# First unit's receptance product from split weights, and a new written order for the first units

## The chip, the cores and the metric

The kernel runs on one core of a Trainium2 chip. The metric is the device time of one execution in microseconds (us). The kernel before took 607.07 us, the median of three runs (606.57 to 607.09). Its engines are TensorE (PE, with its weight loads as PEld), VectorE (DVE), ScalarE (ACT), GpSimd (POOL) and SyncE (SP), which issues every DMA of this kernel.

## What is computed

The reference is sliding-window attention followed by a channel-mixing block. Batch 8, 8 heads, 576 positions, head size 64; window 64; then `d_model` 512 and `d_ff` 1024.

```python
scores = q @ k.T / sqrt(64), kept where 0 <= i - j < 64
attn   = exp(scores - max) / (sum + 1e-9)
x      = attn @ v                       # (8, 576, 512), heads side by side
x_prev = x shifted by one position, first one zero
xk = mu_k * x + (1 - mu_k) * x_prev
xr = mu_r * x + (1 - mu_r) * x_prev
k  = relu(xk @ w_k);  v = (k * k) @ w_v
out = sigmoid(xr @ w_r) * v
```

The weights are stored as 64-bit floats, so the kernel has to turn them into 32-bit ones ("decode") on the chip before it can use them.

## The kernel before, in words

**Units.** The 4608 positions are worked in 9 units of 512 positions (`NU`, `TU`). Each unit has four attention groups g (`NC` = 4 channel chunks of 128), so unit 0 has g0 to g3 and unit 1 has g4 to g7. For one group: scores on PE (`run_s`), per block a masked minimum on DVE (`least`) and an exponential on ACT (`exp`), the reciprocal sums on DVE (`shares`), a scaling on POOL or DVE (`scale`), a transposition of the weights (for unit 0 PE transposes, `flip`, with a copy out on ACT or DVE; later units use DVE's `turn`), the product with v on PE (`run_x`) and the copy of x to SBUF.

**Mixing.** Per unit and chunk c, `mix` (L873) makes xr and xk: `diff` (any of three engines), `blend` (DVE), and, where the product is a split one, `high` (a cast to fp32r, ACT or POOL) and `low` (the rest, a subtraction on DVE or POOL).

**Products.** `product` (L951) makes a 128x512 output from `count` chunks. A *split* product is three fp32r matmuls for each chunk: high weight by high x, high by low, low by high. A *whole* one is one fp32 matmul for each chunk, which needs neither `high` nor `low` of x nor the two parts of the weight; the trace has two records for it. `direct` (L484) decides: with `DIRECT = "rk"` unit 0 takes w_r and w_k whole, and all else is split. Unit 0 has 4 x 4 r products (r0 to r3, chunks c0 to c3), 8 x 4 k products and 4 x 8 v products.

**Weights.** 20 chunks n of 512 KB are loaded: n0 to n3 are w_r, n4 to n11 w_k, n12 to n19 w_v. `decode` (L421) takes each through `sign` (ACT), `clamp` (DVE or POOL), `shift`, `top`, `low` (DVE), then `first_part` (a cast, ACT or POOL) and `second_part` (a subtraction, POOL or DVE), which give the split weight. Where a chunk is used whole in unit 0, `low` writes a tile `whole` that stays, and the two parts are made at any time before unit 1.

**Order.** Every step is a numbered `Piece`. `play` (L206) walks through a model of the engines and gives each engine its order of instructions. For the beginning the orders are written out: `ORDER` (L90) lists for each engine the piece numbers in the order in which it issues them; what is not listed there follows by the model's own choice, with assumed costs. Engines run their own list in order and wait for each other by semaphores. `PLACES` (L81) names the pairs of groups (j, groups 2j and 2j+1) ahead of whose `run_x` PE's instruction addresses are aligned by no-operations. `BOUND` (L46) is the model time up to which a POOL piece is also ordered behind the last DVE piece that shares a port with it.

Of the kernel before, what the change touches and what calls it, by code (L numbers as in the profile page):

```python
# [42 lines left out]
SB = 14  # L43

ORDERED = mybir.DependencyInfo(mybir.DependencyClass.Sync, mybir.DependencyReason.DATA)
BOUND = 125000  # L46

GATES = 1
LATER = (4,)

DIRECT = "rk"
SPLIT = (-9, -47)
WHOLE = 859

# [23 lines left out]
LINK = {"DVE": 125, "ACT": 135, "POOL": 90, "PE": 205, "SP": 80}  # L78
FAR_LINK = 45

PLACES, SKIP = {3: 7, 4: 7, 8: 7, 12: 7, 16: 7}, 12  # L81

RING = 8
FIRST = 730
# [4 lines left out]

ORDER = {  # L90
# [9 lines left out]
    ),  # L100
    "DVE": (
# [11 lines left out]
    ),  # L113
    "ACT": (
# [10 lines left out]
    ),  # L125
    "POOL": (
# [4 lines left out]
    ),  # L131
# [7 lines left out]
    ),  # L139
}  # L140

# [6 lines left out]
def attn_rwkv_kernel(ctx, tc, qT, kT, v2, mu_k, mu_r, w_k, w_v, w_r, out):  # L148
# [57 lines left out]
    def play():  # L206

        left, free, now, begun, port, bus, landed, run = {}, {}, 0, [], 0, 0, [], None
        holder = None
        moved, clock, tiled = 0, [WINDOW, 0, True], None  # L210
# [34 lines left out]
        while any(left.values()) or any(script.values()):  # L245
            assert times, [(e, [(p.key, p.fn.__name__) for _, _, p in ps[:4]]) for e, ps in left.items()]
            now = heapq.heappop(times)
            while ends and ends[0][0] <= now:
                _, _, p = heapq.heappop(ends)
# [4 lines left out]
            for e, ps in left.items():  # L254
# [3 lines left out]
                for _, n, p in ([(0, 0, given[-1])] if given else ps):  # L258
# [37 lines left out]
                    if locks:  # L296
                        port = p.done
# [4 lines left out]
                    if p.size:  # L302
                        early = moved < 1.034e6
                        bus, moved = max(bus, now - 335), moved + p.size
                        bus += 36 + p.size / (352.6 if early else 376.6) + 178 * (early and p.size > 5e5)
                        landed.append(bus + (2132 if early else 3373))
                        p.lag = landed[-1] - p.done + (1500 if bus > 16000 else 300)
                        heapq.heappush(times, landed[-1])
                    if e == "PE":
# [8 lines left out]
    def d1(n):  # L318
        return 65 + 1.04 * n

    def d2(n):
        return 65 + 0.52 * n
# [658 lines left out]
    def r_units(key, u, xr, gate, n=TU):  # L981
        made, hold = [x[2] for x in xr], [x[1] for x in xr]

        for m in range(NC):
            ps, held, p = product(key, wr_s, m, lambda c, e: xr[c][0][0] if e is None else xr[c][0][0][:, e], made, lambda c: [hold[c]], NC, n,
                                  spare=u > 0, u=u)
            state, scratch, result = [], Hold("tmp"), Hold("r")
# [25 lines left out]
            p = Piece("ACT", key, 2 * act_ns(n) + 20, powers, [p], [scratch, result], held)  # L1013
            if u < GATES:
                p = Piece("ACT", key + LATER[0], 2 * cast_ns(n) + 16, bounded, [p])
            p = Piece("DVE", key + (LATER[0] if u < GATES else 0), (0 if u < GATES else 2 * d2(n)) + d1(n), share, [p], uses=[scratch], port=True)
            gate.append((state, result, p))

    def k_units(key, u, xk, k2, n=TU):
# [109 lines left out]
    for j in range(PAIRED // 2, len(groups) // 2):  # L1129
        u = 2 * j // NC  # L1130
# [79 lines left out]
```

## Time and profile before

| what | value |
|---|---|
| median of three runs | 607.07 us (606.57 to 607.09) |
| the profiled execution | 607.59 us |
| its span, first to last instruction | 605.8 us |
| PE busy | 593.6 us (98%) |
| DVE busy | 391.1 us (65%) |
| ACT busy | 371.3 us (61%) |
| POOL busy | 133.9 us (22%) |
| granted TensorE clock, mean | 0.999 |

The span is one execution; 1.79 us of the execution's time lie outside it. Shares are means over the whole span: the stages differ much, with DVE and ACT nearly full over the first 100 us and half empty later. In the views a line is nearly always L168, since all instructions go through one helper there, so the names of the tiles say what a row is: `bank<-xm,whole` is a whole product, `bank<-xs,ws` or `bank<-ks,ws` a split one, `bank<-qk` scores, `bank<-ident,pr` PE transposes, `bank<-pt,v` attention times v.

### The profile page before, as it was taken

The page shows a single profiled execution, that of the slowest core. Times are in us where ns is not written, and L with a number is a line of the kernel's source. Part 1 is how long each engine was busy: PE and PEld are TensorE (multiplying, and loading weights), DVE is VectorE, ACT ScalarE, POOL GpSimd, SP SyncE. Part 2 cuts the span into 40 slices and gives each one's busy share as a digit, 9 for nine tenths or more (in the row PEclk, how much of TensorE's full clock was granted, in tenths as well). Part 3 has the DMA queues.
Part 4 walks back from the last instruction along what each step waited for, and adds up shares of the span by engine and source line. Part 5 has one row for each costly group of instructions (what it writes and reads, how often), then busy time and mean ns, then how long its engine had stood idle before and what let it go on. Part 6 is the DMA issues. An engine that isn't in the chain of part 4 may idle for free.

```text
span 605.8 us, 17561 instructions
## 1 busy us (share of the span) xinstructions
PE 593.6 (98%) x7008; PEld 464.7 (77%) x7008; DVE 391.1 (65%) x1210; ACT 371.3 (61%) x1057; POOL 133.9 (22%) x205
## 2 busy tenths in 40 slices
PE   5999999999999999999999999999999999999997
PEld 4644577888888888888888888887888888888885
DVE  5999999737782768366754677277828683665211
ACT  6898967475576646673577358645865476743620
POOL 6665546202300330022101130023002300201000
PEclk9999999999999999999999999999999999999999
DMA  8988133213221323122312222132212220010001
GB/s 276 320 287 282 47 88 105 80 45 107 83 77 46 93 75 97 40 82 63 110 40 57 88 83 66 41 110 81 75 46 93 92 81 24 3 53 18 0 18 52
DMA packets 56913, 53.32 MB, mean 88 GB/s; under 512 B 10496, under 2 KB 50432, under 8 KB 56832
## 3 DMA queue, kind: packets, MB, share of 16 engines
q1 hardware_dynamic: 56832, 52.20, 28.2%
q8 instruction: 56, 0.92, 0.6%
q14 instruction: 25, 0.20, 0.1%
HBM read 42.73 MB, written 9.44 MB: 86 GB/s over the span
## 4 chain that ended last, share of the span: by engine, by line
PE 84%; DVE 6%; ACT 4%; DMA 3%; SPq 1%; issue 1%; POOL 1%; ACTq 0%
PE bank L168 84%; DVE bank L168 1%; DMA raw<-w_k 1%; ACT pr L168 1%; SPq L168 1%; DMA v<-v 1%; DMA raw<-w_r 1%; DVE xm L168 1%; ACT ws L168 1%; DVE wt L168 1%; ACT kf L168 1%; DVE d L168 1%; DVE r L168 0%; DVE whole L168 0%; DVE pt L168 0%
## 5 line engine op out<-in xcount | busy, mean ns | idle before, releaser
L168 PE MATMUL bank<-xs,ws 128*128 128x512 f32 x1152 | 272.7, 396 | 0.0
L168 PEld LDWEIGHTS bank<-xs,ws 128*128 128x128 f32 x1152 | 215.8, 188 | 51.0
L168 PE MATMUL bank<-ks,ws 128*128 128x512 f32 x864 | 206.8, 398 | 0.1
L168 PEld LDWEIGHTS bank<-ks,ws 128*128 128x128 f32 x864 | 161.3, 188 | 39.5 <-issue 1.0
L168 DVE TENSOR_TENSOR ks<-kf,ks 128x512 fp32r<-128x512 f32 x70 | 51.3, 734 | 93.7 <-ACT ks L168 93.5
L168 ACT ACTIVATE pr<-pr,nmax 128x96 f32<-128x96 f32 (+1 forms) x288 | 105.2, 368 | 8.8 <-DVE nmax L168 8.3
L168 ACT ACTIVATE kf<-bank 128x512 f32<-128x512 f32 x72 | 43.0, 598 | 61.1 <-PE bank L168 60.7
L168 DVE CUSTOM_DVE_ANT_0 pr<-bank,bands 128x96 f32<-128x96 f32 x256 | 49.5, 250 | 14.3 <-PE bank L168 14.3
L168 POOL CAST ks<-kf 128x512 fp32r<-128x512 f32 x7 | 4.3, 612 | 244.9 <-ACT kf L168 206.0
L168 ACT COPY xT<-bank 128x256 f32<-128x256 f32 (+1 forms) x43 | 14.5, 392 | 67.0 <-PE bank L168 67.0
L168 ACT ACTIVATION_READ_ACCUMULATOR pr<-pr,nmax 128x1 f32 x288 | 54.5, 189 | 0.0
L168 ACT ACTIVATE kf<-kf 128x512 f32<-128x512 f32 x71 | 44.8, 633 | 2.0
L168 ACT ACTIVATE th<-bank 128x512 f32<-128x512 f32 x36 | 21.3, 591 | 38.5 <-PE bank L168 27.2
L168 DVE SCALAR_TENSOR_TENSOR r<-bank,r 128x512 f32<-128x512 f32 x36 | 24.4, 680 | 31.4 <-PE bank L168 31.3
L168 PE MATMUL bank<-xm,whole 128*128 128x512 f32 x96 | 43.1, 599 | 0.0
L168 ACT CAST ks<-kf 128x512 fp32r<-128x512 f32 x65 | 40.3, 620 | 2.1 <-POOL kf L168 0.3
L168 PE MATMUL bank<-qk 64*32 64x96 f32 (+1 forms) x2112 | 33.4, 254 | 7.8 <-DMA qk<-kT 5.2
L168 PEld LDWEIGHTS bank<-qk 64*32 64x32 f32 (+1 forms) x2112 | 28.2, 108 | 15.9 <-DMA qk<-qT 5.2
L168 PEld LDWEIGHTS bank<-pt,v 32*64 32x64 f32 (+1 forms) x2656 | 34.3, 130 | 7.0 <-issue 5.0
L168 ACT CAST xs<-d 128x512 fp32r<-128x512 f32 x49 | 28.8, 618 | 15.3 <-POOL d L168 13.7
L168 DVE TENSOR_TENSOR xs<-d,xs 128x512 fp32r<-128x512 f32 x57 | 37.3, 698 | 0.4 <-ACT xs L168 0.4
L168 DVE COPY xT<-bank 128x256 f32<-128x256 f32 x26 | 10.3, 421 | 42.2 <-PE bank L168 42.2
(79 smaller groups left out, 562.0 us busy)
## 6 DMA issues: line engine op xcount, KB each, us to landing
v<-v SPq DMA_DIRECT2D x68, 64.0 KB, 2.0
raw<-w_k SPq DMA_DIRECT2D x8, 512.0 KB, 8.4
raw<-w_v SPq DMA_DIRECT2D x8, 512.0 KB, 6.0
v<-v SPq DMA_DIRECT2D x60, 48.0 KB, 2.0
raw<-w_r SPq DMA_DIRECT2D x4, 512.0 KB, 4.8
outT<-r SPq DMA_DIRECT2D x8, 256.0 KB, 2.0
v<-v SPq DMA_DIRECT2D x60, 32.0 KB, 1.9
qk<-kT SPq DMA_DIRECT2D x8, 224.0 KB, 3.7
```

The source lines that it names most:

```text
L168: self.last = tc.keep_in_program_order(op(*args, **kw))
```

## The change

The first unit's r product takes split weights, as in all later units: `DIRECT` goes from "rk" to "k". So `mix` makes `high` and `low` for the four xr of unit 0 (8 pieces more, ACT and DVE by the new order), the chunks n0 to n3 are no longer kept as `whole` tiles, and their `first_part` and `second_part` have to be there before the first r product. All piece numbers above 1487 move by up to 8. The written order of all five engines is new and reaches further (PE 166 pieces where it had 135, into unit 1's v product). In the written order of after:

- PE: scores g0, g1, flip g0, scores g2, flip g0, x g0, flip g1 h0, scores g3, flip g1 h1, x g1, **flip g2 h1**, then r0 c0, r1 c0, r2 c0, r3 c0 (1510, 1517, 1524, 1531), flip g2 h0, scores g4, x g2, two r products of c1, flip g3 h1, one of c1, flip g3 h0, scores g5, x g3, the other nine r products, then k. Before, the four c0 products (1502, 1509, 1516, 1523) stood right behind x g1, and eight r products ahead of x g3.
- DVE: the small `rest` (40) first; `low` of xr0 to xr3 (1489, 1493, 1497, 1501) and `second_part` of n3 and n2 among the first 80; three `least` of g3 stand ahead of `low` of xr0. The scaling of g1 h1 and of g2 h0, `second_part` of n1 and a few `clamp` leave DVE; the scaling of g3 h1 comes to it.
- ACT: `high` of xr0 to xr3 (1488, 1492, 1496, 1500), the `diff` of xr1 and xr2, and `first_part` of n1, n3, n2.
- POOL: `second_part` of n0 (11) ahead of the scaling of g1, that of g1 h1 (554) ahead of the `diff` of xr0, then the scaling of g2 and `second_part` of n1 (23).
- SP: the two 2 KB loads of mu_k and mu_r (38, 39) third and fourth, between k and q of g0's first half; before, they stood behind the second weight chunk.

The rest: `PLACES`, `BOUND` and two costs of the model (the landing time of a load and the price of `share`, which affect only the order that `play` chooses behind the written one).

```diff
-BOUND = 125000
+BOUND = 130000
-DIRECT = "rk"
+DIRECT = "k"
-PLACES, SKIP = {3: 7, 4: 7, 8: 7, 12: 7, 16: 7}, 12
+PLACES, SKIP = {4: 7, 7: 7, 11: 7, 15: 7}, 12
 ORDER = {
     "PE": (
-        509, 510, 535, 531, 566, 533, 559, 561, 557, 555, 590, 563, 1502, 1509, 1516, 1523, 588, 586, 645, 614,
-        1503, 1510, 612, 1524, 1517, 610, 667, 616, 1511, 1525, 1518, 1504, 1505, 1526, 1512, 1519, 1530, 1531,
+        509, 510, 535, 531, 566, 533, 559, 561, 555, 590, 557, 563, 588, 1510, 1517, 1524, 1531, 586, 645, 614,
+        1511, 1532, 612, 1525, 610, 667, 616, 1518, 1519, 1512, 1526, 1533, 1513, 1527, 1520, 1534, 1538, 1546,
...
     "DVE": (
-        6, 7, 511, 513, 517, 521, 515, 525, 527, 523, 519, 8, 9, 529, 544, 536, 548, 540, 538, 550, 546, 542, 19,
-        532, 20, 552, 567, 554, 575, 571, 581, 579, 577, 569, 573, 40, 21, 1487, 599, 591, 605, 31, 595, 593, 601,
-        583, 32, 603, 597, 584, 33, 589, 1489, 23, 607, 646, 654, 648, 48, 658, 660, 49, 656, 650, 50, 652, 64, 55,
+        40, 6, 7, 511, 515, 513, 517, 521, 8, 525, 519, 523, 527, 9, 529, 544, 536, 550, 548, 542, 546, 538, 540,
+        532, 19, 20, 567, 552, 569, 575, 571, 577, 573, 581, 579, 21, 562, 556, 31, 599, 583, 1487, 605, 591, 32,
+        1489, 595, 597, 601, 593, 33, 1491, 48, 603, 49, 50, 1493, 607, 646, 609, 650, 654, 652, 660, 658, 64, 648,
...
     "POOL": (
-        643, 520, 10, 18, 530, 553, 30, 565, 1486, 644, 585, 1488, 22, 47, 609, 608, 63, 618, 1490, 51, 11, 1492,
+        643, 520, 10, 18, 530, 11, 553, 30, 565, 554, 1486, 585, 47, 584, 644, 23, 63, 618, 608, 55, 1498, 1502, 87,
...
     "SP": (
-        4, 1, 0, 2, 3, 12, 13, 16, 38, 25, 27, 39, 24, 15, 14, 28, 631, 633, 41, 42, 26, 43, 619, 44, 620, 634, 622,
+        4, 0, 38, 39, 1, 2, 3, 13, 12, 16, 25, 15, 24, 28, 14, 42, 26, 633, 41, 619, 45, 27, 622, 43, 631, 634, 620,
...
-                        landed.append(bus + (2132 if early else 3373))
+                        was = moved - p.size
+                        landed.append(bus + (2132 if was < 7.8e5 else 2750 if was < 1.2e6 else 3373))
...
-            p = Piece("DVE", key + (LATER[0] if u < GATES else 0), (0 if u < GATES else 2 * d2(n)) + d1(n), share, [p], uses=[scratch], port=True)
+            p = Piece("DVE", key + (LATER[0] if u < GATES else 0), (0 if u < GATES else 2 * d2(n) + 140) + d1(n), share, [p], uses=[scratch], port=True)
```

## Rows read from the trace of the kernel before

**Rows 1.** The page: busy us (share of the span) and instructions of each engine.

```profile
PE 593.6 (98%) x7008; PEld 464.7 (77%) x7008; DVE 391.1 (65%) x1210; ACT 371.3 (61%) x1057; POOL 133.9 (22%) x205
```

**Rows 2.** Chain of waits that ended last: start us, us, what; its last long piece.

```profile
92.80 509.43 PE bank L168 x4956
```

**Rows 3.** What PE waited for, 0 to 150 us: us, times, longest us.

```profile
PE bank L168 <- ACT kf L168: 0.5, 1, 0.5
PE bank L168 <- ACT pt L168: 0.4, 2, 0.2
PE bank L168 <- DVE wt L168: 0.3, 1, 0.3
```

**Rows 4.** Stretches: length, then busy us and instructions of each engine, clock, DMA.

```profile
15.00:20.00 5.00, 4.60 (x105) 3.75 (x102) 4.66 (x29) 4.77 (x17) 2.44 (x5) 1.00 1.02 347
35.00:40.00 5.00, 5.00 (x13) 2.13 (x13) 4.96 (x10) 5.00 (x12) 2.90 (x4) 1.00 0.91 261
```

**Rows 5.** Timeline of PE: start us, us, what, count, [idle before <- releaser].

```profile
9.12 1.99 PE L168 MATMUL bank<-qk 64*64 64x128 f32 x32 [1.58 <-DMA qk<-qT]
...
17.73 1.10 PE L168 MATMUL bank<-qks 64*64 64x128 f32 x32
18.76 1.15 PE L168 MATMUL bank<-pt,v 128*64 128x64 f32 x32
19.84 3.70 PE L168 MATMUL bank<-xm,whole 128*128 128x512 f32 x8
23.38 1.04 PE L168 MATMUL bank<-ident,pr 128*128 128x128 f32 x8
...
33.44 17.43 PE L168 MATMUL bank<-xm,whole 128*128 128x512 f32 x40
...
100.07 22.48 PE L168 MATMUL bank<-xs,ws 128*128 128x512 f32 x96
```

**Rows 6.** Timeline of DVE, the same columns.

```profile
11.16 0.29 DVE L168 CUSTOM_DVE_ANT_0 pr<-bank,mask 128x128 f32<-128x128 f32 x1 [0.41 <-PE bank L168]
...
12.86 0.69 DVE L168 TENSOR_SCALAR bank<-wt 128x512 uint32<-128x512 uint32 x1
13.46 0.68 DVE L168 COPY pt<-bank 128x512 f32<-128x512 f32 x1
...
18.70 0.75 DVE L168 SCALAR_TENSOR_TENSOR xm<-xT,mur,xm 128x512 f32<-128x512 f32 x1 [0.34 <-POOL xm L168]
19.37 0.28 DVE L168 CUSTOM_DVE_ANT_0 pr<-bank,mask 128x128 f32<-128x128 f32 x1
...
50.75 0.68 DVE L168 SCALAR_TENSOR_TENSOR whole<-raw,bank 128x512 uint32<-128x512 uint32 x1
```

**Rows 7.** Timeline of SP's DMA issues: start us, us, what.

```profile
1.16 0.43 SPq L168 DMA_DIRECT2D qk<-qT  x1
1.64 0.90 SPq L168 DMA_DIRECT2D qk<-kT  x2
```

**Rows 8.** Groups of instructions: busy us, mean ns of one, idle before them.

```profile
L168 ACT CAST xs<-d 128x512 fp32r<-128x512 f32 x49 | 28.8, 618 | 15.3 <-POOL d L168 13.7
L168 DVE TENSOR_TENSOR xs<-d,xs 128x512 fp32r<-128x512 f32 x57 | 37.3, 698 | 0.4 <-ACT xs L168 0.4
```

**Rows 9.** Timeline of POOL, the columns of rows 5.

```profile
16.04 1.04 POOL L168 TENSOR_TENSOR pr<-pr,rs 128x512 f32<-128x512 f32 x1 [2.90 <-DVE pr L168]
...
32.14 1.28 POOL L168 TENSOR_TENSOR ws<-whole,ws 128x512 fp32r<-128x512 f32 x1 [0.67 <-DVE xm L168]
...
35.03 1.18 POOL L168 TENSOR_SCALAR wt<-wt 128x512 f32<-128x512 f32 x1
36.83 0.61 POOL L168 TENSOR_SCALAR wt<-wt 128x512 f32<-128x512 f32 x1 [0.63 <-DVE xm L168]
```

**Rows 10.** Timeline of PE in the later units, the columns of rows 5.

```profile
167.75 1.73 PE L168 MATMUL bank<-qk 64*32 64x96 f32 x128
...
327.64 1.84 PE L168 MATMUL bank<-qk 64*32 64x96 f32 x128
```

70 rows, old and new, of the table ORDER are left out of this document.

## The prediction

> **What bounds the kernel now.** I read the shares first: PE is busy 98% of the span, the next engine 65% [rows 1]. Then the chain that ended last: from 92.80 us on it is one piece of PE for 509.43 us without a break [rows 2]. So behind 93 us only PE's own work counts, and nothing that another engine does there moves the end. Ahead of it the waits of PE say how much of the beginning is not PE's: beside the loads at the start they are 0.5, 0.4 and 0.3 us [rows 3]. The stretches show that this closeness is not comfort: from 15 to 20 us PE, DVE and ACT are each at 92 to 95%, and from 35 to 40 us all three at 99% or more [rows 4]. So the end is PE's work plus PE's waits in the first 90 us, and DVE and ACT decide those waits as soon as they get more to do or PE gets less. Short gaps don't all show as waits, since the ends of matmuls are modelled; I therefore reckon with starts.
>
> **What PE gains.** 20 whole products run from 33.44 us in 17.43 us, 0.87 us each, and 32 split ones (96 matmuls) in 22.48 us, 0.70 each [rows 5]. The 16 r products of unit 0 are worth 16 x 0.17 = 2.7 us.
>
> **What it costs at the first r product.** It is a new wait. Before, r0 c0 needs only the blended xr0; DVE has it at 19.37, and the four products of c0 start at 19.84, right behind x g1 [rows 5, 6]. After, they wait for DVE's `low` of xr0, and behind them in PE's queue stand the flip of g2 h0, scores g4 and x g2, for which ACT's copies and DVE's next `least` wait. When does `low` come? DVE's list from the first `least` of g1 to that `low` is: 19 `least`, at (12.86 - 11.16)/8 = 0.21 each, 4.0 us; eight full-size steps (two copies, shift and top of n1, low of n1, shift and top of n2, `low` itself), at 13.46 - 12.86 = 0.60 each, 4.8 us; the blend, 19.37 - 18.70 = 0.67; two `shares` and a half-size copy, 1.0 together (an estimate: each between a `least` and a full step). Sum 10.5 us [rows 6]. The same durations for before's list from 11.16 to the end of the blend give 7.9, and the trace has 8.2, of which 0.34 is a wait for POOL [rows 6], so the method holds to 0.1.
>
> The start of that list: mu_k, mu_r now stand ahead of q of g0, and one issue takes 0.47 us [rows 7], so scores g0 and g1 are issued two places later. The scores of g1 waited for their q at 9.12 [rows 5], when several loads were in flight; the delay lies between 0 (the DMA engines are the limit) and 0.94 (the issue is). DVE's `rest` now waits for those loads too, with DVE's whole list behind it, which then has idle time to give before 11.16. I take 0.3, nearest to the full DMA engines. So `low` ends at 11.16 + 0.3 + 10.5 = 21.95, and with 0.15 for the signal the first r product starts at 22.1, 2.26 us later than before.
>
> **The sum to the first k product.** Before, it starts at 33.44 + 8 x 0.87 = 40.4 us [rows 5]. From the first r product on that is 20.55 us. After, the same stretch lacks 2.7 us of r work, the flip of g2 h1 (moved ahead; 1.04/2 = 0.5 us [rows 5]) and the 0.4 us of waits for `pt` there if they go [rows 3]: 16.9, so 22.1 + 16.9 = 39.0. What is late next: xr3's `low`. The list puts it at about 36.4 on DVE, with second_part n2 waiting behind ACT's cast; PE wants it at 36.2, so 0.2 more. First k at 39.2, a gain of 1.2 us.
>
> The other new work: four casts on ACT (618 ns) and four subtractions on DVE (698 ns) [rows 8], 2.5 us and 2.8 us as they are shown, less where they overlap. They are in the lists just summed. The second parts of n0 and n1 on POOL (1.28 each) come earlier, at no cost while POOL has gaps such as the 2.90 us ahead of its scaling at 16.04 [rows 9]; without those gaps each would delay x g1 by its full 1.28. Replacing `whole` pairs by split xr pairs leaves as many big tiles in use, four, so I reckon no wait for memory.
>
> **From the first k product to the end.** Two waits of before, 0.5 for `kf` and 0.3 for `wt` [rows 3], stand in a decode and a softmax chain that the new order moves; gone, they give 0.8. A new one is possible at k4 c1, the 18th k product of the new order, at 39.2 + 17 x 0.87 = 54.0. It needs chunk 9, whose last step ended at 51.4 before [rows 6]; by the durations above DVE's list up to it sums to 46.1 us where it was 42.7, 3.4 more (2.5 of it the four `low`), and it starts with 0.4 less idle: about 54.4, a wait of 0.4. A list summed over 46 us can be off by 1 us, so the wait lies between 0 and 1.4; I count 0.3, near what the sum says. Net gain 0.5. Sum: -1.2 - 0.5 = -1.7 us. The profiled execution took 607.59, 0.52 above the median; I take the difference from the median: 607.07 - 1.7 = 605.4.
>
> The places of alignment are bounded from both sides: scores of a pair take 1.73 us or 1.84 [rows 10], thirteen pairs in the dense part, so at most 13 x 0.11 = 1.4 us either way; six of the thirteen take 1.8 or more, so the room is -0.7 to +0.8, and I take nothing. `BOUND` and the two model costs change the order behind the written lists, where only PE counts [rows 2]: nothing, unless PE is made to wait there, where now there is none.
>
> **A rule against the change.** POOL's clamp at 35.03 took 1.18 us where the same took 0.61 at 36.83 [rows 9]; the new `low` steps on DVE read two operands from SBUF and so add such meetings. By the Trainium skill, SBUF — State Buffer, section "Who interferes with whom", a VectorE instruction with two SBUF inputs holds the shared ports against a GpSimd one that reads SBUF for its whole length, and the other is fully blocked. The trace agrees in kind; if all four `low` blocked POOL for their length, POOL would lose about 2.8 us by rows 8, and the sum would only change where POOL's result is waited for.
>
> **The rivals.**
> 1. *The rest hides the late start.* x g1 itself comes later in the new order (its copy of g1 stands behind a cast on ACT) and `low` is there when PE arrives; no chunk is late. Then all of 2.7 plus the waits of 1.2 [rows 3] less the shorter start: -3.0, 604.1. For it: DVE's list may start without the 0.3. Against: 10.5 us of DVE work without a gap.
> 2. *PE's clock falls.* The column of the granted clock says 1.00 throughout [rows 4], yet 32 score matmuls took 1.99 us at 9 us and 1.10 at 17.7 us [rows 5], near the ratio of the two levels 1.2 and 2.4 GHz; ahead of the first of these PE had waited 1.58 us for a load. The new order leaves PE some 2 us idle between 19 and 22 us. If it falls, x g1 or the four r products (2.8 us) run up to 1.8 times as long: 0.9 to 2.2 us, 606.3 to 607.6, I take 607.2. Against: PE's gaps before were longer. The Trainium skill, TensorE: Matmul & The Clock Gate, section "What's actually happening", has the throttled state as the default and activity as what lifts it; the two rows of scores agree.
> 3. *Slower: POOL's queue is late with xr0.* Second part of n0 (1.28) and the scaling of g1 h1 (1.04) now stand ahead of the `diff` of xr0 on POOL. By durations it ends 0.3 us before DVE wants to blend. If four POOL steps there each lose 0.6 to a DVE step, as the clamp at 35.03 did [rows 9], and the scaling of g1 so holds up x g1 as well, the first r product starts 2.1 us later or more, and each us is one of PE. From 1.7 us on the gain is gone, from 2.9 on it is slower by more than can be told; with x g1's own 1.1 us pushed behind as well it is 605.4 + 3.2 = 608.6. Against: POOL's gap of 2.90 us [rows 9].
> 4. *No change.* PE waits in turn for each half of w_r and xr, as DVE and ACT are at 99% [rows 4]: the 2.7 us become waits, 607.0.
>
> **How the numbers follow.** Forecast 0.46, within 604.6 to 606.2; rival 1 0.13; 2 0.17; 3 0.14; 4 0.10. About 0.2%, 1.2 us, is what a measurement tells from no change, so faster means below 605.86, slower above 608.28. Faster: three quarters of the forecast and all of rival 1, 0.48. Slower: most of rival 3 and a little of 2, 0.15. The rest, 0.37, is no difference. The range leaves out less than one part in ten on each side: below, half of rival 1, 603.7; above, the worse half of rival 3, 608.3.
>
> **What would show it.** Split r products of 0.70 us; the first of them at 22.1 (20.5 to 23.5) behind a wait for DVE's xs; the first whole k product at 39.2; a small wait at chunk 9; the long last piece of PE in the chain starting no later than 93 us. The forecast is wrong if the r products run longer than 0.75, if the first starts behind 24, if PE shows more than 1.5 us of waits between 40 and 100, or if the pairs of scores in the dense part leave their 1.73 to 1.84 us.

## The result

The changed kernel is slower: 612.29 us median (611.86 to 613.25, four runs) against 606.82 (606.35 to 607.09, four runs) for the kernel before; the ratio is 1.0092, with a 95% interval of 1.0079 to 1.0105. The forecast was 605.4, and 612.29 lies outside its range. The profiled execution took 611.92 us, its span is 610.1, 4.3 more than the 605.8 of before.

The page of the kernel after, busy us (share of the span) and instructions, against [rows 1]:

```profile
PE 593.1 (97%) x7024; PEld 469.2 (77%) x7024; DVE 391.9 (64%) x1209; ACT 374.2 (61%) x1063; POOL 138.3 (23%) x208
```

PE works no longer than before; the time is in its gaps. Its waits over the whole span (us, times, longest us), against [rows 3], the first row mostly the loads at the start:

```profile
PE bank L174 <- DMA qk<-qT: 7.8, 3, 6.1
PE bank L174 <- issue: 1.3, 1, 1.3
PE bank L174 <- ACT pt L174: 0.8, 1, 0.8
PE bank L174 <- POOL pr L174: 0.7, 2, 0.6
PE bank L174 <- ACT kf L174: 0.7, 1, 0.7
```

The chain that ended last (start us, us, what): the long last piece of PE, which began at 92.80 [rows 2], now begins at 187.74. Ahead of it stand two pieces of PE with a gap of 1.34 us between them, and from 161.35 to 187.74 us the chain goes through DVE and ACT (cut here).

```profile
75.34 20.61 PE bank L174 x278
95.95 1.34 issue
97.29 64.06 PE bank L174 x647
...
187.74 418.82 PE bank L174 x4010
```

The timeline of PE (start us, us, what, count, [idle before <- releaser]); the first r product comes 3.4 us later than at 19.84 and the first k product, in spite of shorter r products, 0.4 later than at 40.4 [rows 5]:

```profile
21.07 1.15 PE L174 MATMUL bank<-pt,v 128*64 128x64 f32 x30 [0.85 <-ACT pt L174]
22.78 0.66 PE L174 MATMUL bank<-ident,pr 128*128 128x128 f32 x4 [0.57 <-POOL pr L174]
23.19 3.03 PE L174 MATMUL bank<-xs,ws 128*128 128x512 f32 x12
...
34.41 6.60 PE L174 MATMUL bank<-xs,ws 128*128 128x512 f32 x27
40.84 5.74 PE L174 MATMUL bank<-xm,whole 128*128 128x512 f32 x13
...
75.34 0.98 PE L174 MATMUL bank<-qk 64*32 64x96 f32 x62 [0.70 <-ACT kf L174]
...
93.19 2.07 PE L174 MATMUL bank<-pt,v 32*64 32x96 f32 x160
95.18 0.77 PE L174 MATMUL bank<-qk 64*32 64x96 f32 x41
97.29 1.28 PE L174 MATMUL bank<-qk 64*32 64x96 f32 x87 [1.34 <-issue]
...
159.28 2.07 PE L174 MATMUL bank<-pt,v 32*64 32x96 f32 x160
...
179.12 2.01 PE L174 MATMUL bank<-qk 64*32 64x96 f32 x120 [1.47 <-DMA qk<-qT]
...
187.74 1.93 PE L174 MATMUL bank<-pt,v 32*64 32x96 f32 x148 [0.50 <-DVE nmax L174]
```

**Where the time went.** Waits alone don't add up, so I keep an account of PE: *lost time* at a point is the start of a piece there less all the work that PE has issued up to it, at one price for each kind of matmul in all kernels (0.234 us for a split one, 0.434 for a record of a whole one, 1.99 for the values of a pair, 1.66 for its scores, all from start to start). It is worked out from the whole timeline of one execution; it can be off by 0.3 us.

| lost us at | first k product | 112 us | 200 us | last product | work of PE |
|---|---|---|---|---|---|
| before | 12.4 | 14.4 | 14.5 | 16.9 | 585.4 |
| after | 15.5 | 18.5 | 21.6 | 23.9 | 582.7 |
| more in after | 3.1 | 1.0 | 3.0 | -0.1 | -2.7 |

(The third row is what each stretch adds.) The sum, 3.1 + 1.0 + 3.0 - 0.1 - 2.7 = 4.3, is the difference of the spans. So the split saves its 2.7 us, the front takes it back, and the stretch from 112 to 200 us, of which the forecast said nothing, costs the most that was not expected.

### The profile page after: what moved, and what is told of

Read it like the earlier page. It is cut to its first block, busy times and chain, and to the rows that moved or that the text cites. A ratio compares the mean times of both kernels' runs of the same rounds, so it can differ in the third digit from the quotient of the medians.

```text
span 610.1 us, 17607 instructions
## 1 busy us (share of the span) xinstructions
PE 593.1 (97%) x7024; PEld 469.2 (77%) x7024; DVE 391.9 (64%) x1209; ACT 374.2 (61%) x1063; POOL 138.3 (23%) x208
## 4 chain that ended last, share of the span: by engine, by line
PE 83%; DVE 7%; DMA 5%; issue 1%; ACT 1%; SPq 1%; POOL 0%; DVEq 0%; ACTq 0%
PE bank L174 83%; DMA raw<-w_v 3%; DVE pr L174 1%; DVE d L174 1%; DMA qks<-kT 1%; DMA raw<-w_k 1%; SPq L174 1%; DVE r L174 1%; ACT pr L174 1%; DMA raw<-w_r 1%; DVE bank L174 1%; DVE xs L174 1%; DVE pt L174 1%; DVE th L174 0%; ACT ks L174 0%
## 5 line engine op out<-in xcount | busy, mean ns | idle before, releaser
L174 PE MATMUL bank<-xs,ws 128*128 128x512 f32 x1200 | 285.5, 396 | 0.0
L174 PEld LDWEIGHTS bank<-xs,ws 128*128 128x128 f32 x1200 | 224.4, 188 | 53.2 <-DVE xs L174 0.2
L174 ACT ACTIVATE pr<-pr,nmax 128x96 f32<-128x96 f32 (+1 forms) x288 | 105.1, 367 | 17.4 <-DVE nmax L174 16.9
L174 DVE TENSOR_TENSOR ks<-kf,ks 128x512 fp32r<-128x512 f32 x65 | 46.8, 720 | 89.6 <-ACT ks L174 88.7
L174 DVE SCALAR_TENSOR_TENSOR r<-bank,r 128x512 f32<-128x512 f32 x36 | 24.5, 682 | 39.4 <-PE bank L174 39.2
L174 PE MATMUL bank<-qk 64*32 64x96 f32 (+1 forms) x2112 | 34.5, 254 | 10.5 <-DMA qk<-qT 7.8
L174 ACT ACTIVATE kf<-kf 128x512 f32<-128x512 f32 x69 | 43.5, 631 | 1.9
L174 ACT CAST xs<-d 128x512 fp32r<-128x512 f32 x53 | 31.6, 616 | 13.7 <-POOL d L174 11.7
L174 PE MATMUL bank<-pt,v 32*64 32x96 f32 (+3 forms) x2656 | 37.5, 245 | 1.5 <-ACT pt L174 0.8
```

The lines of the kernel that those rows point to most:

```text
L174: self.last = tc.keep_in_program_order(op(*args, **kw))
```

## The experiments

Each ratio is to runs of the kernel before on the same chip; "over" is the ratio's excess times 607 us. The kernel after is 5.6 us over in these terms (4.8 to 6.4). A list of piece numbers was kept as after (or before) has it on all engines, and only what the diff shows was moved.

### What the order does alone, and which half of it

`e4_order_alone`: the new order with whole r products.

```
-DIRECT = "k"
+DIRECT = "rk"     # and the 8 high and low pieces of xr leave ORDER
```

> The kernel after's order of every engine with the first unit's r products whole as in the kernel before, and without the eight pieces (four casts on ACT, four subtractions on DVE) that make high and low parts of xr0 to xr3: what the new order does alone. Theory (the split saves its 2.7 us of PE and the order loses about 7): 612.3 plus 2.7 less what the missing high and low parts give back at the front (0 to 2 us): 613.0 to 615.0. Rival (the split itself is what costs, through its late parts at the front, and the order costs little): 607 to 609.

Measured: 614.76 us, ratio 1.0125 (1.0107 to 1.0142), 7.6 over. As the theory had it: PE's work is 585.4 us again and the lost time (15.9 at the first k product, 23.5 at the end) is that of after within 0.4. So the split does what it says, and the order alone costs about 7 us. The front is late with no `low` in it too, but this execution doesn't say by how much: the granted clock fell to 0.50 in it from 17.2 to 20.6 us, where 32 score matmuls took 1.76 us in place of 1.10, which is worth about 1.5 us (an estimate from the three pieces of PE there and the same pieces at full clock). The one run with the clock at 1.00 throughout took 613.89 us, 6.5 over.

`e6_new_front` has after's order up to the first k product and before's from there; `e8_old_front` has it the other way round, with whole r products.

```
 e6: each engine's list = after's pieces up to u0 k0 c0, then before's
 e8: each engine's list = before's pieces up to u0 k0 c0, then after's (whole r)
```

> Split r products and the kernel after's order on every engine up to the first k product (40.8 us), and from there the kernel before's order on every engine. Theory (the new order loses 3 us of PE up to the first k product, which eats the split's 2.7, and 3.9 us behind it, by the lost time of the two traces: 8.3 behind it in after, 4.4 in before): 3.9 us less than after, 1.0 to 2.2 us over the kernel before. Rival (the late front itself makes the later waits, because DVE and ACT stay behind): 4 us and more over before.

> Whole r products and the kernel before's order on every engine up to the first k product (40.4 us), and from there the kernel after's order on every engine (without the high and low parts of xr0 to xr3): what the later part of the new order does alone. Theory: its waits at the scores of groups 7, 8, 9, 14 and 15 are there as in the kernel after, 3.9 us over the kernel before (3.0 to 5.0). Rival (these waits come from the late front): within 1 us of the kernel before.

Measured: 613.48 us, 1.0107 (1.0089 to 1.0125), and 614.73, 1.0115 (1.0084 to 1.0147): e6 is 6.5 over, as its rival said, and e8 7.0, which neither said. At the seam each makes waits of its own (`whole` from DVE, 1.98 and 1.62 us at 46.7; in e6 the granted clock fell to 0.50 behind it, in e8 behind another wait at 77 us), so the totals don't weigh the halves. One thing they do tell apart: from 112 to 200 us the kernel with before's later order loses 0.2 us, the one with after's 3.0. That loss belongs to the later order and not to the late front.

### 112 to 200 us: q and k loads ahead of v loads

`e5_g14_back` moves the scores whose wait is shown at 179 us.

```
 "PE" (from u2's first k products on):
-1874, 924, 946, 1875, ...
+1874, 1875, ... 1933, 924, 946     # other engines by the planner's rule
```

> The kernel after with its order kept on every engine up to the scores of groups 12 and 13, and with the scores of groups 14 and 15 put back on PE to where the kernel before has them, behind u2's last k product (about 20 us later); what the other engines do from there on follows the planner's rule. Theory (behind the written lists the planner put these scores before their q load could have landed, and PE waits 1.5 us at 179 us and 0.5 us at 187 us for it): these waits go, 2.2 to 3.1 us less, which leaves 2.4 to 3.3 us over the kernel before (after alone: 5.5). Rival (PE is late there for DVE's or ACT's work, and any other piece put in that place waits as long): 4.5 to 5.5 us over before.

Measured: 612.42 us, 1.0090 (1.0070 to 1.0110). The theory falls: the wait for q goes, but PE waits 1.59 us for DVE's xs and 0.66 for its pt in the same place, and from 112 to 200 us it loses 3.1. The wait named in the view was only the one that came last. The stretch before it shows why. DMA issues of SP, first of the kernel after, then of the kernel before:

```profile
112.33 0.43 SPq L174 DMA_DIRECT2D v<-v  x1
141.00 0.80 SPq L174 DMA_DIRECT2D qk<-kT  x2
141.85 0.91 SPq L174 DMA_DIRECT2D qk<-qT  x2
142.80 2.08 SPq L174 DMA_DIRECT2D v<-v  x2
144.92 0.43 SPq L174 DMA_DIRECT2D qk<-kT  x1
145.40 10.29 SPq L174 DMA_DIRECT2D v<-v  x22
```

```profile
124.07 8.14 SPq L168 DMA_DIRECT2D v<-v  x16
137.51 0.85 SPq L168 DMA_DIRECT2D qk<-kT  x2
```

In after, SP's list has loads of q and k for groups 12 and 13 ahead of 24 v loads for groups 10 and 11. The first of them has to wait for a buffer that the scores of groups 10 and 11 give free at 141.0 us. SP runs its list in order, so the v loads stand behind it from 112 to 141 us, and they need nothing of what it waits for: in the next run they are issued from 113.9 to 135.4 us. The values that need them come at 159.28 in place of 151.6 us, and the other engines run dry. Two stretches of ten microseconds of the kernel after (length, then busy us and instructions of PE, PEld, DVE, ACT, POOL, clock, DMA):

```profile
150.00:160.00 10.00, 10.00 (x104) 7.97 (x104) 1.38 (x2) 0.00 (x0) 0.00 (x0) 1.00 0.48 143
...
170.00:180.00 10.00, 8.48 (x85) 6.47 (x87) 8.93 (x46) 10.00 (x41) 2.20 (x5) 1.00 0.48 134
```

DVE and ACT are nearly idle from 150 to 160 us and full from 170 to 180, where PE stands. `e9_v_first` puts the v loads first:

```
 "SP":
-230, 229, 232, 231, 221, 215, 241, 227, ... 225, 237, 1779,
+221, 215, 227, ... 225, 237, 230, 229, 232, 231, 241, 1779,
 "PE":
-1793, 1794, ... 1804, 866, 867, 1805,
+1793, 866, 867, 1794, ... 1804, 1805,
 "DVE":
-1798, 869, 871, 1820, 1821,
+869, 871, 1820, 1821, 1798,
```

> The kernel after with its order kept up to the scores of groups 12 and 13, but for three things that belong together: on SP the 17 v loads of groups 10 and 11 that stand behind five q and k loads of groups 12 and 13 go ahead of these, as in the kernel before; on PE the values of groups 10 and 11 go nine products earlier, behind u1 v2 c3, where the kernel before has them; on DVE the copies of their result go ahead of u1's third gated output. From there on every engine follows the planner's rule. Theory (in after those five loads wait until the scores of groups 10 and 11 have run at 141.0 us, and hold the v loads behind them in SP's queue from about 122 to 155.7 us; so the values come at 159.3 instead of 152 us, DVE and ACT stand idle from 150 to 160 us, and u2's x comes late: the 2.4 to 3.1 us that PE loses at 177 to 188 us): v loads issue from about 122 us, no PE wait over 0.3 us between 130 and 200 us, 2.2 to 3.1 us less than after, which leaves 2.4 to 3.3 us over the kernel before. Rival (DVE as a whole is full there, and the wait moves on, as it did when the scores of groups 14 and 15 were put back): 4.5 to 5.6 us over before.

Measured: 608.88 us, ratio 1.0034 (1.0021 to 1.0046), 2.1 over (the v loads are 24, not 17). The v loads and the values that need them in e9, and these values in the kernel before:

```profile
113.91 21.49 SPq L180 DMA_DIRECT2D v<-v  x25
155.25 2.06 PE L180 MATMUL bank<-pt,v 32*64 32x96 f32 x160
```

```profile
151.62 2.06 PE L168 MATMUL bank<-pt,v 32*64 32x96 f32 x160
```

PE shows no wait from 130 to 200 us and loses 0.3 there; in five more kernels below that carry this edit it is 0.1 to 0.3, and in eight with after's later order 3.0 to 3.3 (5.5 in one whose clock fell there). This is the largest cause, 3.5 us of the 5.6 by the two ratios and 3.0 by the lost time, and it is shown.

### The stretch without a releaser at 97 us

`e1_apart` puts one product ahead of each of the two scores; `e3_before_together` takes the products out between them and the values in the kernel before.

```
 e1 "PE": -764, 765, 771, 793, 1626, 1627,
          +764, 765, 1626, 771, 1627, 793,
 e3 "PE": -764, 765, ... 1600, 1618, 771, 793,
          +764, 765, 771, 793, ... 1600, 1618,
```

> The kernel after with its order kept on every engine, but for two pieces of PE: the scores of groups 8 and 9 stand behind the r and v products that followed them (one product of u0's v2 ahead of each) instead of directly behind the values of groups 6 and 7. Theory (PE runs out of instructions when 320 short matmuls of values and 256 of scores stand in one row with nothing long between them): the idle 1.34 us inside the scores at 95.95 us, which the trace puts to no releaser, goes, and the span falls by 1.0 to 1.6 us (610.1 to about 608.8), 611.0 us where the kernel after takes 612.3. Rival (a data wait or a bank that the trace does not name): the same idle time stands inside the scores where they now are, and the time is within 0.4 us of the kernel after.

> The kernel before with its order kept on every engine, but for two pieces of PE: the scores of groups 8 and 9 are put directly behind the values of groups 6 and 7, as the kernel after has them (before, eight products of 5.6 us stand between). Theory (instructions run out): an idle stretch of 1.0 to 1.6 us with no releaser appears inside the scores, and the total rises from 606.8 to about 608.0. Rival (the stall of the kernel after comes from what its other engines do there): no such stretch, the total within 0.4 us of 606.8, or a wait with DVE or ACT as releaser.

Measured: 612.52, 1.0085 (1.0070 to 1.0100); and 617.50, 1.0169 (1.0152 to 1.0186). In e1 the stretch shrank to 0.49 us, but PE then waits for DVE, and at 112 us it has lost 18.4, as after: no gain. (The 320 and 256 of the expectation count the weight loads with the matmuls, of which there are 160 and 128.) e3 (which skips eleven products, not eight) doesn't answer its question: DVE's list isn't made for early scores, and PE waits 2.37 and 3.02 us for its copies and decodes, 7.0 us in all from 83 to 92 us. It shows how dear one wrong place is: 10 us. Not all of it is waits: behind them the granted clock was 0.50 from 88 to 97 us.

`e14_v_mu_apart` (with e9's edit and the one of e7 below) puts three products between:

```
 "PE": -764, 765, 771, 793, 1626, 1627, 1682,
       +764, 765, 1626, 1627, 1682, 771, 793,
```

> As the run with the v loads first and the mu loads back, and with three products (u0 v2 c4, c5 and u1 r0 c0, nine split matmuls, 2.1 us) between the values of groups 6 and 7 and the scores of groups 8 and 9. Theory (PE's instructions run out in 576 short instructions on end, and arrive 2.5 us after the transfer that brings them has begun): no idle stretch without a releaser over 0.3 us between 90 and 105 us, the scores of group 8 end within 0.6 us of where they ended with the stall, and 0.9 to 1.4 us come off: 0 to 0.6 us over the kernel before. Rival (DVE gets the scores later and gives u1's x later, as in the run with one product between): within 0.4 us of the run without this edit.

Measured: 609.53 us, 1.0042 (1.0029 to 1.0055), the same as e13 without the edit, below. PE in e14, in its longest run (611.64 us; the four others took 609.10 to 609.58, the five of e13 609.14 to 610.39, so a gain of some tenths is not excluded):

```profile
71.34 1.58 PE L180 MATMUL bank<-pt,v 32*64 32x96 f32 x115
74.99 0.90 PE L180 MATMUL bank<-pt,v 32*64 32x96 f32 x45 [2.08 <-issue]
...
94.88 2.06 PE L180 MATMUL bank<-pt,v 32*64 32x96 f32 x160
96.87 1.66 PE L180 MATMUL bank<-ks,ws 128*128 128x512 f32 x6
98.36 0.86 PE L180 MATMUL bank<-xs,ws 128*128 128x512 f32 x3
99.16 1.73 PE L180 MATMUL bank<-qk 64*32 64x96 f32 x128
...
105.54 0.72 PE L180 MATMUL bank<-xs,ws 128*128 128x512 f32 x2 [0.60 <-DVE xs L180]
```

The mechanism holds: with long matmuls between, all 128 score matmuls run in one piece of 1.73 us. The gain doesn't: PE waits for u1's xs instead, and this execution has a stretch of the same kind at the other place where values and scores (of groups 4, 5 and 7) stand together. What points to the supply of instructions is the queue that carries them. In the kernel after, from 94 to 95 us (queue: transfers, MB, share of 16 engines), there is one transfer, and none from 90 to 94 or from 95 to 98:

```profile
q8 instruction: 1, 0.02, 5.8%
```

It begins at 94.97, and PE goes on at 97.29. There are 17 stretches of over 0.4 us without a releaser behind the first 10 us, in after and 14 of the experiments, and in every one PE goes on 2.2 to 2.7 us after such a transfer begins, of which a kernel has only 56. Before, e3 and e6, with before's order there, have none. No run changes the supply alone, so this stays an inference. Why e14 and e8 have the stretch in the values at 75 us and the others don't is open; e4 has 160 values and 64 scores on end there without one.

`e16_places` undoes the edit of `PLACES` alone.

```
-PLACES, SKIP = {4: 7, 7: 7, 11: 7, 15: 7}, 12
+PLACES, SKIP = {3: 7, 4: 7, 8: 7, 12: 7, 16: 7}, 12
```

> The kernel after with the kernel before's places at which PE's instructions are aligned (ahead of the values of pairs 3, 4, 8, 12 and 16 in place of 4, 7, 11 and 15), its order as it is. Theory (alignment moves the instructions by a few places only; the steady pairs of scores took 1.73 to 1.86 us and the values 2.06 in both traces): within 0.5 us of the kernel after, 5.0 to 5.9 us over before, the idle stretch at 97 us still there and longer than 1 us. Rival (this edit of the change is what lets the instructions run out): the stretch goes or halves, 4.0 to 4.7 us over before.

Measured: 614.19 us, 1.0117 (1.0099 to 1.0135); the stretch is there with 1.37 us, and another of 0.57 comes at 223 us. The edit of `PLACES` is not a cause: with this order the old places are no better, and with 7.1 over the total is above what either side forecast.

### The front

`e7_mu_back` puts the mu loads and `rest` where before has them; `e17_flip_behind` (with e9's edit) moves the first flip of group 2 behind the four first r products.

```
 e7  "SP":  -4, 0, 38, 39, 1, 2, 3, 13, 12, 16, 25, 15,
            +4, 0, 1, 2, 3, 13, 12, 16, 38, 25, 15, 39,
     "DVE": -40, 6, 7, ... 579, 21,
            +6, 7, ... 579, 40, 21,
 e17 "PE":  -588, 1510, 1517, 1524, 1531, 586,
            +1510, 1517, 1524, 1531, 588, 586,
```

> The kernel after with the two mu loads back where the kernel before issues them on SP (behind the second weight load, not ahead of three of the first q and k loads) and DVE's two operations on them behind the masks of group 2, not first in its list. Theory (they hold up the q and k loads and with them the scores of group 2 by 0.62 us): PE's lost time at the first r product falls from 14.4 us by 0.6 to 0.9 us, the total by as much, 4.6 to 4.9 us over before. Rival (the first r product waits for the low part of xr0, which DVE ends at 23.27 us whatever PE does): the first r product starts at 23.2 us as now, the total unchanged within 0.3 us, 5.2 to 5.8 over before.

> The kernel after with the v loads of groups 10 and 11 first (2.1 us over the kernel before), and at the front one piece of PE moved: the first flip of group 2 behind the four first r products, where the kernel before has it, not ahead of them. Theory (the first r products wait for that flip, which waits 0.5 to 0.8 us for POOL's scaling, and the low part of xr0 has come by then): they start at 22.3 to 22.6 us in place of 23.1, the first k product and the end 0.4 to 0.8 us earlier, 1.3 to 1.8 us over the kernel before. Rival (low comes last, at 23.2 us, and the flip only filled the gap): the r products start at 23.0 us or later, the flip and all behind it come later, the end 0.3 us or more later, 2.4 us and more over before.

Measured: e7 611.70 us, 1.0082 (1.0057 to 1.0107). The first r product comes at 22.19 and the lost time at the first k product is 14.5 (after 15.5; 15.1 in e1 and e5, which have after's front), so 0.6 to 1.0 us in this execution. But executions scatter as much: the first r product starts at 22.19 to 22.93 in four kernels with this edit (e7, e11, e13, e14) and at 22.64 to 23.48 in eight with after's front. About half a microsecond is left, and in the total that is within the interval. e17: 612.35, 1.0088 (1.0069 to 1.0107), over 3 us worse than e9: the rival holds. About 1.6 us of this is the clock's in the profiled execution, which had it at 0.50 from 23.6 to 27.0 us (an estimate: 11 split matmuls took 4.37 us there, 12 took 3.03 in after); the run with the highest clock, 0.999, took 611.47 us, still 4.2 over. PE and DVE in e17:

```profile
22.26 0.49 PE L180 MATMUL bank<-xs,ws 128*128 128x512 f32 x1
23.51 4.37 PE L180 MATMUL bank<-xs,ws 128*128 128x512 f32 x11 [0.76 <-DVE xs L180]
...
31.52 1.15 PE L180 MATMUL bank<-pt,v 128*64 128x64 f32 x32 [1.84 <-ACT pt L180]
```

```profile
22.28 1.17 DVE L180 TENSOR_TENSOR xs<-d,xs 128x512 fp32r<-128x512 f32 x1
```

The first matmul needs only `high` of xr0 and runs at 22.26; the next needs `low`, which ends at 23.45. So `low` is last, as the prediction had it, and the flip filled the gap. With the flip behind, its copy, the values of group 2 and all else come later.

### Scores of group 7, and the repairs together

`e2_g7_later` moves the scores of group 7 two products on; `e10_relu_early` moves the relu whose bank they wait for two pieces forward on ACT. `e11_three` has the edits of e9, e7 and e10, `e12_four` also moves ACT's copy of group 1's flip ahead of the first part of chunk 1, `e13_v_mu` has those of e9 and e7.

```
 e2  "PE":  -690, 742, 1614, 1615,    +690, 1614, 1615, 742,
 e10 "ACT": -1591, 158, 1584, 1598,   +1591, 1598, 158, 1584,
 e12 "ACT": -22, 558,                 +558, 22,
```

> The kernel after with one piece of PE moved: the scores of group 7 stand two v products (u0 v1 c2, c3; six split matmuls, 1.4 us) later than directly behind the values of groups 4 and 5. Theory (the scores take a PSUM bank that ACT's relu of a k output frees at 75.3 us; 0.70 us of idle time): the wait goes, PE's lost time by 80 us falls by 0.7 to 1.0 us, the total to about 611.4 us. Rival (the wait is only the first of a chain, and the next product or PE's next bank is late by as much): the lost time by 100 us is the same and the total stays at 612.3 (within 0.4).

> The kernel after with one piece of ACT moved: the relu of u0's last k output stands two pieces earlier, ahead of the sign of weight chunk 17 and the cast of k5. Theory (PE's 0.70 us of idle time in the scores of group 7 at 75.3 us is the wait for the bank that this relu frees, and the relu stands behind 1.3 us of ACT work that nobody is waiting for): the idle time goes, lost time by 80 us 0.5 to 1.0 us less, the total 4.5 to 5.0 us over the kernel before. Rival (the next stage sets the pace, and the time is lost again by 110 us, as in the run that moved the scores): 5.3 to 5.7 us over before.

> The three repairs together: the v loads first with the values of groups 10 and 11 earlier, the mu loads back in their old place, and the relu of k7 two pieces earlier. Theory (each takes away its own wait): 2.7 + 0.8 + 0.7 = 4.2 us less than after, 0.6 to 2.2 us over the kernel before. Rival (one wait is hidden by the next): 3 us and more over before.

> The three repairs and a fourth: on ACT the copy of the first flip of group 1 (pt) goes ahead of the first part of weight chunk 1, which stood before it. Theory (the first r product waits for the low part of xr0, which DVE ends last, so an earlier pt only lets PE wait later): the wait for pt falls from 0.85 us to under 0.3 us, the first r product starts within 0.3 us of where it does without the fourth repair, the total is the same within 0.4 us. Rival (PE's own order is what is late at the front): the first r product and the total come 0.5 to 0.9 us earlier.

> The kernel after with the v loads of groups 10 and 11 first (and their values nine products earlier) and with the mu loads in their old place, without the relu move, whose wait only went to the next piece (1.6 us for ACT's xT at 78 us). Theory (the two add up): 2.1 us over the kernel before, which the v loads alone left, less 0.5 to 0.9: 1.2 to 1.6 us over. Rival (the front's waits are not on the path to the end): 2.0 us over or more.

| run | us | ratio (95%) | what follows |
|---|---|---|---|
| e2 | 614.65 | 1.0117 (1.0091 to 1.0142) | the wait goes, PE waits for ACT's xT at 77.5 |
| e10 | 612.78 | 1.0097 (1.0084 to 1.0110) | the wait goes, 1.61 for xT at 78.1 comes |
| e11 | 610.03 | 1.0048 (1.0036 to 1.0060) | 2.9 over, no better than the 2.1 of e9 alone |
| e12 | 609.80 | 1.0056 (1.0044 to 1.0068) | the wait for pt goes, 1.99 for POOL's pr comes |
| e13 | 610.25 | 1.0041 (1.0027 to 1.0054) | 2.5 over: with the mu loads back no better than e9 |

At 70 to 80 us ACT is busy 9.33 of 10 us, so a piece taken from its place there only hands the wait on, as the rivals of e2 and e10 said. e2 is 7.1 over, more than its rival had: in its profiled execution PE waits 2.6 us for q from 178 to 181 us, and the granted clock is 0.50 behind it. Of all repairs only the v loads gain more than the noise, and no version beats the kernel before.

## Why the prediction was wrong

**The split's gain** was right: 2.7 us by PE's work (585.4 to 582.7), and the total of e4 is 2.0 us above that of after.

**The first r product** was right in kind and too early: 22.1 forecast, 23.19 measured. DVE in the kernel after:

```profile
11.51 0.26 DVE L174 CUSTOM_DVE_ANT_0 pr<-bank,mask 128x128 f32<-128x128 f32 x1
...
16.40 0.29 DVE L174 CUSTOM_DVE_ANT_0 pr<-bank,mask 128x128 f32<-128x128 f32 x1 [0.38 <-PE bank L174]
...
22.10 1.17 DVE L174 TENSOR_TENSOR xs<-d,xs 128x512 fp32r<-128x512 f32 x1
```

The list began at 11.51, as forecast (11.46), but took 11.8 us to the end of `low` and not 10.5. `low` itself was priced at 0.60, the step from start to start of a DVE instruction, and took 1.17, since POOL was scaling from 21.68 on:

```profile
21.68 1.04 POOL L174 TENSOR_TENSOR pr<-pr,rs 128x512 f32<-128x512 f32 x1 [1.96 <-DVE nmax L174]
```

POOL ends at 22.72, and `low` ends 0.55 us later, about its own length. It is the same in all 14 kernels with the split: the scaling begins 0.4 us ahead of `low`, and `low` takes 1.15 to 1.19 us. The prediction had the meeting of the two engines, but only as something that delays POOL. The Trainium skill, SBUF — State Buffer, section "Who interferes with whom", says that it is the order of issue that decides who blocks; the two rows agree, POOL having begun first. Another 0.38 is a wait for PE; the last 0.3 I can't place. The wait for PE is not in every execution: in after PE still ran as at the lower of the clock's two levels at 15.14 us (a flip took 1.11 us), in e1, with the same front, a flip at 14.70 took 0.66, DVE shows no such wait, and the first r product starts at 22.75.

**The first k product** came at 40.84, not 39.2: 1.1 us from the first r product and 0.5 on the way. In lost time the front was to cost 1.5 us and cost 3.1. e4, with no `low`, lost 15.9 there; less the 1.5 for its clock that is 14.4, still 2.0 more than before. So the late `low` is not the whole of it, by this estimate the smaller part: DVE, ACT and POOL are ordered there so that something else is late when it isn't. Which piece of the order costs most is open; e7, e12 and e17 took away single waits, and others came.

**From the first k product to 112 us** a gain of 0.5 was forecast, and it is a loss of 1.0. The wait for kf didn't go (0.70 in place of 0.5), that for chunk 9 didn't come, and the stretch of 1.34 us at 97 us could not be read from the trace of before, where no values and scores stand together in that place.

**Behind the written lists: "nothing, unless PE is made to wait there".** This step failed most. "Behind 93 us only PE's own work counts" was read from a chain that shows what was late in the old order; it doesn't show how much room the other engines had. The cause stands in the diff: SP's new list is longer, and it puts loads that wait for a buffer ahead of loads that don't. The step counted PE, DVE, ACT and POOL and left SP's queue out, and so put at nothing what measured 3.0 us of lost time from 112 to 200 us.

**The rivals.** Not one was it. The 3.0 of rival 1 doesn't follow from its terms: 2.7 and 1.2 are 3.9, and no row gives the 0.9 taken off for "the shorter start". In the kernel after the granted clock, once up, stayed at 1.00, against rival 2 (it came up later: the flip at 15.14 us took 1.11 us, in before the one at 14.20 took 0.66); in e4, e12 and e17 it did fall at the front. Rival 3 had the place (POOL and DVE at xr0) but not the size. The forecast's own marks of failure came: over 1.5 us of waits between 40 and 100 us, and a last long piece that begins behind 93.

## What to carry to other kernels

When a written order changes, go through the DMA queue's list as through the engines': for each load, what must have run before its buffer is free, and what stands behind it. A chain of one engine without a gap says nothing about how near the others are; where a wait is removed and the total stays, look for an earlier stretch in which the other engines were idle.

## What the runs showed of the hardware

**Short matmuls on end can outrun PE's instructions.** In 15 places where 160 value matmuls and 64 or 128 of scores, each with its own weight load, stood on end (3 to 3.7 us of work), PE stood idle 1.15 to 2.08 us with no releaser, and went on 2.2 to 2.7 us after a transfer of instructions had begun; with 2.3 us of long matmuls between them (e14) it did not stand there. Not every such place has it (e4 at 75 us).

**A wait of PE can cost twice.** In e9 PE stood 1.72 us at 97 us, and then the granted clock fell to half (length, busy us, clock, DMA as above):

```profile
98.00:99.00 1.00, 1.00 (x87) 0.99 (x87) 0.51 (x5) 0.84 (x2) 0.00 (x0) 1.00 0.00 0
99.00:100.00 1.00, 1.00 (x20) 0.72 (x4) 1.00 (x4) 0.00 (x0) 0.00 (x0) 0.75 0.06 16
100.00:101.00 1.00, 1.00 (x4) 0.81 (x3) 1.00 (x3) 0.00 (x0) 0.00 (x0) 0.50 0.66 185
...
103.00:104.00 1.00, 1.00 (x6) 0.82 (x5) 1.00 (x8) 1.00 (x4) 0.37 (x3) 1.00 0.96 364
```

Six split matmuls took 2.64 us there, 1.66 at full clock, and PE lost 1.7 us more by 103 us. That execution took 611.69 us, the five others of the same kernel 608.57 to 609.32. It fell also behind waits of 1.97 (e8), 1.98 (e6), 1.99 (e12) and 2.08 us (e14), and where shorter ones came one behind another, the last of 1.27 (e2), 1.21 (e4) and 0.76 us (e17). It did not behind those of 1.34 (after), 1.63 (e7), 1.64 (e13) and 1.84 us (e17, at 31.5 us). So the length of the last wait alone doesn't tell whether it falls. The Trainium skill, TensorE: Matmul & The Clock Gate, section "What's actually happening", has 1.2 GHz as the state that activity lifts to 2.4; the 0.50 behind a pause agrees.
